# Padding two small tiles so that the tiles behind them begin at other addresses

## The chip, the cores and the metric

The program runs on one core of a Trainium2 chip. The metric is device time in microseconds, the median of several executions; lower is better. One further execution was recorded by the hardware profiler, and all rows below come from it.

## The reference, cut to what matters

```python
def reference(q, k, v, tau, moe_*, moe2_*):
    # 1. sparse attention: 4 batches x 8 heads, 576 tokens, head size 64
    scores = q @ k.T / 8;  keep scores >= rowmax - tau;  softmax;  attn @ v
    # 2. first layer, 2304 tokens x 512, inner width 1024
    x = ((x @ w1) * (x @ w2)) @ w3 @ w_out
    # 3. router and experts: 8 experts, inner width 1024
    P = exp(x @ w_gate - max); 8 rounds of normalising rows and columns
    out = sum over e of P[:, e] * (relu(x @ w1[e]) @ w2[e])
```

All arrays are float32.

## The kernel before, in words

**Arithmetic.** The large products run on TensorE in a float32 mode that takes one pass, and to keep the accuracy each operand is split into a high part and a low part. A product is three matmuls: high by high, high by low, low by high. Every one of these matmuls loads its own stationary operand of 128 by 128.

**Stages.** Attention takes some 390 us; the weights of the first layer are meanwhile converted and multiplied together (w3 by w_out) in its gaps. Then come 120 *units*. Units 0 to 23 are the first layer and units 24 to 119 the experts: three blocks of 768 tokens, eight experts, four parts of the inner width.

**One unit.** It has seven slots. In each slot `mm1` (L692) does six matmuls with 384 moving columns: stationary is a slice of the unit's converted first weights (`w1h`, `w1l`), moving is one of seven combinations of quarter blocks of x (`xh`, `xl`); the results go to the banks `px` and `py`. These are seven products in place of eight. The results are combined (`combine`), rectified and split into `hh` and `hl`, and one unit later the second product runs from a queue (`mm2`, L762) between the slots: for the experts 512 moving columns of `w2h` or `w2l` against stationary slices of `hh` and `hl`; for the first layer the roles are exchanged, with 256 or 512 moving columns. The result is added up in the banks `ye`.

**Preparation.** For the next unit `prep1` (L607 to L619) makes the converted first weights on GpSimd and ScalarE from a 512 KB load (`raw1`), and `prep2` makes `w2h` and `w2l` on ScalarE and VectorE. The order of all instructions is written out by hand. SyncE issues all transfers.

**Memory.** Tiles come from pools that are stacked from two ends. From the left: `const` (first `ntau`, then x), `moe` (sums of x, the even units' `w1h` and `w1l`, and `wt`), the converter's tiles during attention and in their place the `xh` and `xl`, then `moe1` (`prob`, `wg`, `ca`, `raw1`, the odd units' `w1h` and `w1l`, temporaries), then `moe2` (`raw2`, `acc`, `hh`, `hl`, `w2h`, `w2l`). From the right: all of attention's own tiles and the w3 by w_out tiles. Right-hand pools close before left-hand ones open over their place, and a tile opened there waits for the work on the tiles that it covers. Each tile begins at a multiple of 32 bytes in its partition, so `ntau`, which holds one number, takes 32 bytes. In units of bytes per partition, `prob` takes 576 and `wg` 128.

The two tiles that the change pads are `ntau`, L983 (the threshold, loaded once at L295, negated at L308, and read at L150 as the bias of a ScalarE operation in attention), and `wg`, L558 (the router's weights, loaded once at L559 and read at L843 as the moving operand of the 144 small matmuls of the router).

Of the kernel before, what the change touches and what calls it, by code (L numbers as in the profile page):

```python
# [9 lines left out]
F32 = mybir.dt.float32  # L10
# [10 lines left out]
DM, DFF, E = 512, 1024, 8  # L21
# [494 lines left out]
class Moe:  # L516
# [37 lines left out]
    def grow(self):  # L554

        pool = self.pool = self.odd = self.stack.enter_context(self.k.tc.tile_pool(name="moe1", bufs=1))
        self.p = pool.tile([128, NCH, E], F32, name="prob")
        self.wg = pool.tile([128, 4, E], F32, name="wg")  # L558
        self.nc.sync.dma_start(self.wg, self.k.wg)  # L559
        self.ca = pool.tile([128, 4, HT], F32, name="ca")  # L560
        self.load1(1)
# [413 lines left out]
@with_exitstack  # L975
def kernel(ctx, tc, qk, vv, tau, w1, w2, w3, wo, wg, e1, e2, out):
    k = Ctx()
    k.tc, k.nc = tc, tc.nc
    nc = tc.nc
    ctx.enter_context(tc.manual_schedule())  # L980
    const = ctx.enter_context(tc.tile_pool(name="const", bufs=1))
    dram = ctx.enter_context(tc.tile_pool(name="scratch", bufs=1, space=bass.MemoryType.DRAM))
    k.ntau = const.tile([128, 1], F32, name="ntau")  # L983
    k.tau = tau
    k.x = const.tile([128, 4, NTOK], F32, name="x")
    k.qk, k.vv, k.w3, k.wo, k.wg, k.w1, k.w2, k.out = qk, vv, w3, wo, wg, e1, e2, out
    k.w64 = {"a": w1, "b": w2}
    k.w34 = dram.tile([4, 128, 2, DM], F32, name="w34")
    k.wab = {n: dram.tile([4, 128, 1024], F32, name=f"w_{n}") for n in ("a", "b")}
    k.xk = dram.tile([3, 7, 128, 2 * HT], F32, name="x_low")  # L990
    k.wk = dram.tile([8, 2, 128, 7 * 256], F32, name="w_kept")
    attention(k)
# [44 lines left out]
```

## Time and profile before

| | |
|---|---|
| median of 3 executions | 2190.81 us (2189.88 to 2191.28) |
| the profiled execution, device time | 2189.07 us |
| its span, first to last instruction | 2187.3 us |
| busy share: PE, PEld, DVE, ACT, POOL | 98%, 86%, 58%, 43%, 48% |
| granted TensorE clock, mean | 1.000 |

PE stands for TensorE's matmuls, PEld for its weight loads, DVE for VectorE, ACT for ScalarE, POOL for GpSimd, SP for SyncE. A matmul's duration in the trace reaches from its start to the modelled end of its result, so that successive matmuls overlap; the distance of their starts tells the rate.

### The profile page before, as it was taken

The numbers are of one execution on the slowest core, as the hardware profiler recorded it, in microseconds if no ns is written. First come the engines' busy times: TensorE is split into PE (matmuls) and PEld (weight loads), VectorE is DVE, ScalarE is ACT, GpSimd is POOL, SyncE is SP. The second block draws the span as 40 slices with busy tenths as digits, with TensorE's granted clock in tenths as the row PEclk, the third lists the DMA queues.
The fourth block names the chain that finished last, engine by engine and source line by source line (L and its number), as shares of the span: only waits on it lengthen the run. The fifth ranks groups of instructions, "written<-read, shape, count | busy, mean of one in ns | idle before, by whom it ended". The sixth has DMA issues, their size and how long they took to land.

```text
span 2187.3 us, 31994 instructions
## 1 busy us (share of the span) xinstructions
PE 2150.1 (98%) x12496; PEld 1872.5 (86%) x12496; DVE 1274.8 (58%) x2122; ACT 948.0 (43%) x1770; POOL 1042.4 (48%) x1018
## 2 busy tenths in 40 slices
PE   7999999999999999999999999999999999999999
PEld 4666666899999899999998999999998999999998
DVE  7888888765555654454556445454546444545454
ACT  7888887442324333333334333333334333333332
POOL 6665657740003444444456545454456444444441
PEclk9999999999999999999999999999999999999999
DMA  4333442775552212121212121212112221212121
GB/s 154 105 128 123 133 139 86 260 264 188 222 199 105 78 58 77 59 77 59 77 58 93 72 77 58 77 59 77 64 72 73 92 72 63 77 59 78 58 77 39
DMA packets 64183, 218.09 MB, mean 100 GB/s; under 512 B 6944, under 2 KB 11040, under 8 KB 64032
## 3 DMA queue, kind: packets, MB, share of 16 engines
q1 hardware_dynamic: 64032, 216.05, 28.0%
q8 instruction: 98, 1.61, 0.3%
q14 instruction: 53, 0.43, 0.1%
HBM read 185.61 MB, written 30.41 MB: 99 GB/s over the span
## 4 chain that ended last, share of the span: by engine, by line
PE 90%; DVE 7%; ACT 2%; issue 1%; POOL 0%; DMA 0%; SPq 0%; ACTq 0%; DVEq 0%; POOLq 0%
PE ye L762 40%; PE py L692 22%; PE px L692 17%; PE s L143 4%; PE pv L241 2%; PE t L187 2%; DVE p L162 2%; DVE nmx L147 2%; PE w L474 1%; DVE cva L506 1%; PE py L843 0%; PE tt L198 0%; ACT e L155 0%; DVE cva L503 0%; PE rb L271 0%
## 5 line engine op out<-in xcount | busy, mean ns | idle before, releaser
L762 PE MATMUL ye<-w2l,hh 128*128 128x512 f32 x1152 | 450.6, 391 | 0.0
L762 PE MATMUL ye<-w2h,hl 128*128 128x512 f32 x1152 | 450.5, 391 | 0.0
L762 PE MATMUL ye<-w2h,hh 128*128 128x512 f32 x1152 | 449.6, 390 | 0.0
L757 ACT ACTIVATE hh<-c 128x384 fp32r<-128x384 f32 x288 | 151.2, 526 | 621.4 <-DVE c L736 621.4
L619 POOL TENSOR_TENSOR w1l<-wt,w1h 128x1024 fp32r<-128x1024 f32 x104 | 253.2, 2434 | 267.2 <-ACT w1h L616 267.1
L692 PE MATMUL py<-xh,w1h 128*128 128x384 f32 x960 | 322.6, 336 | 2.4 <-DVE c L736 1.2
L692 PE MATMUL py<-xh,w1l 128*128 128x384 f32 x960 | 322.1, 336 | 0.0
L692 PE MATMUL py<-xl,w1h 128*128 128x384 f32 x960 | 321.9, 335 | 0.0
L614 POOL TENSOR_TENSOR w1l<-raw,w1h 128x256 fp32r<-128x256 f32 x104 | 80.4, 773 | 471.2 <-ACT w1h L608 457.8
L762 PEld LDWEIGHTS ye<-w2h,hl 128*128 128x128 f32 x1152 | 216.2, 188 | 40.5
L762 PEld LDWEIGHTS ye<-w2l,hh 128*128 128x128 f32 x1152 | 216.3, 188 | 35.3 <-DVE w2l L642 0.3
L692 PE MATMUL px<-xh,w1h 128*128 128x384 f32 x720 | 242.0, 336 | 1.5 <-ACT p L716 1.5
L762 PEld LDWEIGHTS ye<-w2h,hh 128*128 128x128 f32 x1152 | 216.3, 188 | 30.7
L692 PE MATMUL px<-xl,w1h 128*128 128x384 f32 x720 | 241.6, 336 | 0.0
L692 PE MATMUL px<-xh,w1l 128*128 128x384 f32 x720 | 241.5, 335 | 0.0
L607 POOL TENSOR_TENSOR wt<-raw 128x512 f32<-128x512 f32 x104 | 140.8, 1354 | 198.0 <-DMA raw<-in_e 183.0
L758 DVE SCALAR_TENSOR_TENSOR hl<-c,hh 128x384 fp32r<-128x384 f32 x288 | 189.3, 657 | 9.5
L692 PEld LDWEIGHTS py<-xh,w1h 128*128 128x128 f32 x960 | 180.3, 188 | 14.8 <-DVE c L736 3.5
L692 PEld LDWEIGHTS py<-xl,w1h 128*128 128x128 f32 x960 | 180.3, 188 | 7.7
L736 DVE TENSOR_TENSOR c<-px,v 128x384 f32<-128x384 f32 x108 | 60.0, 556 | 212.8 <-PE px L692 212.7
L692 PEld LDWEIGHTS py<-xh,w1l 128*128 128x128 f32 x960 | 180.3, 188 | 0.0
L758 DVE SCALAR_TENSOR_TENSOR hl<-px,hh 128x384 fp32r<-128x384 f32 x96 | 53.4, 556 | 215.5 <-ACT hh L757 215.4
(144 smaller groups left out, 3941.0 us busy)
## 6 DMA issues: line engine op xcount, KB each, us to landing
raw<-in_e SPq DMA_DIRECT2D x192, 512.0 KB, 4.0
wraw<-in_w SPq DMA_DIRECT2D x32, 512.0 KB, 4.0
w1h<-w_kept SPq DMA_DIRECT2D x16, 896.0 KB, 5.2
w1l<-w_kept SPq DMA_DIRECT2D x16, 896.0 KB, 7.0
rq<-in_qk SPq DMA_DIRECT2D x15, 576.0 KB, 5.7
w_kept<-w1h SPq DMA_DIRECT2D x8, 896.0 KB, 8.2
w_kept<-w1l SPq DMA_DIRECT2D x8, 896.0 KB, 9.3
raw<-w SPq DMA_DIRECT2D x12, 512.0 KB, 3.6
```

What stands on the lines that cost most here:

```text
L143: nc.tensor.matmul(out[:, c, 0:KH], lhsT=q[rows, g, cols], rhs=kk[rows, g], start=True, stop=True)
L147: nc.vector.tensor_reduce(out=nmx[:, s % 18:s % 18 + 1], in_=ps[:, :, 0:288], axis=AX.XY, op=ALU.max, negate=True)
L162: nc.vector.scalar_tensor_tensor(out=ppool[g][:, i, 0:S].rearrange("p (a b) -> p a b", a=2), in0=ps[:, :, 0:288], scalar=thr[:, s % 18:s % ...
L187: nc.tensor.transpose(ps[:, c], p[:, 128 * c:128 * c + 128], k.ident)
L607: nc.gpsimd.tensor_tensor(out=t[:, 0:2], in0=raw[:, 1:3], in1=raw[:, 0:2], op=ALU.subtract)
L614: nc.gpsimd.tensor_tensor(out=wl[:, 0], in0=raw[:, 0], in1=f32(wh[:, 0]), op=ALU.subtract)
L619: nc.gpsimd.tensor_tensor(out=wl[:, 3:7], in0=t, in1=f32(wh[:, 3:7]), op=ALU.subtract)
L692: self.nc.tensor.matmul(out, lhsT=w[:, wi, o], rhs=x[xi][:, d], start=n == 0 and not adds, stop=n == 5, skip_group_check=True)
L736: tt(out=c, in0=src, in1=add, op=ALU.add)
L757: nc.scalar.activation(hi, src, AF.Relu)
L758: self.later.append(lambda: nc.vector.scalar_tensor_tensor(out=lo, in0=src, scalar=0.0, in1=f32(hi), op0=ALU.max, op1=ALU.subtract))
L762: self.queue.append((out.shape[-1], lambda: self.nc.tensor.matmul(out, lhsT=l, rhs=r, start=start, stop=stop, skip_group_check=True)))
```

## The change

The two tiles become wider, and the kernel goes on with the same leading part of each. `ntau` grows from 1 to 32 columns of four bytes, that is from 32 to 128 bytes, and `wg` from 4 by 8 to 6 by 8, from 128 to 192 bytes. Everything else is the same text.

```diff
@@ grow
         self.p = pool.tile([128, NCH, E], F32, name="prob")
-        self.wg = pool.tile([128, 4, E], F32, name="wg")
+        self.wg = pool.tile([128, 6, E], F32, name="wg")[:, 0:4]
         self.nc.sync.dma_start(self.wg, self.k.wg)
@@ tile_sparse_attention__then__two_moe_kernel
-    k.ntau = const.tile([128, 1], F32, name="ntau")
+    k.ntau = const.tile([128, 32], F32, name="ntau")[:, 0:1]
     k.tau = tau
```

## Rows read from the trace of the kernel before

**Rows 1.** The page: busy us (share of the span) and instructions of each engine.
```profile
PE 2150.1 (98%) x12496; PEld 1872.5 (86%) x12496; DVE 1274.8 (58%) x2122; ACT 948.0 (43%) x1770; POOL 1042.4 (48%) x1018
```

**Rows 2.** The page: the chain of waits, share of the span by engine and line.
```profile
PE 90%; DVE 7%; ACT 2%; issue 1%; POOL 0%; DMA 0%; SPq 0%; ACTq 0%; DVEq 0%; POOLq 0%
PE ye L762 40%; PE py L692 22%; PE px L692 17%; PE s L143 4%; PE pv L241 2%; PE t L187 2%; DVE p L162 2%; DVE nmx L147 2%; PE w L474 1%; DVE cva L506 1%; PE py L843 0%; PE tt L198 0%; ACT e L155 0%; DVE cva L503 0%; PE rb L271 0%
```

**Rows 3.** By stretch: length, busy us of PE, PEld, DVE, ACT, POOL, clock, DMA.
```profile
0.00:440.00 440.00, 407.99 (x3514) 286.00 (x3515) 369.88 (x727) 342.86 (x736) 282.70 (x419) 1.00 0.43 140
...
900.00:1300.00 400.00, 399.74 (x2011) 361.69 (x2010) 202.08 (x295) 144.82 (x246) 202.66 (x157) 1.00 0.21 73
```

**Rows 4.** Waits after 440 us, all engines, then PE alone: us in total, times, longest.
```profile
POOL w1l L614 <- ACT w1h L608: 452.5, 95, 5.4
POOL w1l L619 <- ACT w1h L616: 264.7, 97, 3.9
...
POOL wt L607 <- DMA raw<-in_e: 183.0, 1, 183.0
...
POOL w1l L614 <- DMA raw<-in_e: 13.4, 1, 13.4
...
PE py L692 <- DVE c L736: 0.5, 2, 0.3
PE px L877 <- DVE small L874: 0.4, 1, 0.4
```

**Rows 5.** Timeline, PE, the last matmuls: start us, duration us, engine, line, operation.
```profile
2179.64 0.39 PE L762 MATMUL ye<-w2h,hl 128*128 128x512 f32 x1
...
2183.04 0.39 PE L762 MATMUL ye<-w2h,hl 128*128 128x512 f32 x1
```

**Rows 6.** Timeline, PE, one slot of an expert unit and what follows it.
```profile
1226.99 0.33 PE L692 MATMUL py<-xh,w1h 128*128 128x384 f32 x1
...
1228.03 0.39 PE L762 MATMUL ye<-w2h,hl 128*128 128x512 f32 x1
```

**Rows 7.** Groups by line: xcount | busy us, mean ns of one | idle before.
```profile
L762 PE MATMUL ye<-w2l,hh 128*128 128x512 f32 x1152 | 450.6, 391 | 0.0
...
L762 PE MATMUL ye<-hh,w2l 128*128 128x256 f32 (+1 forms) x192 | 51.2, 338 | 0.9 <-DVE w2l L642 0.9
...
L692 PE MATMUL py<-xl,w1h 128*128 128x384 f32 x960 | 321.9, 335 | 0.0
...
L692 PE MATMUL px<-xl,w1h 128*128 128x384 f32 x720 | 241.6, 336 | 0.0
```

**Rows 8.** Timeline, DVE, three masks of attention in a row (the accumulators' reads left out).
```profile
86.90 0.81 DVE L162 SCALAR_TENSOR_TENSOR p<-s,thr,e 128x576 f32<-128x576 f32 x1
...
89.46 0.80 DVE L162 SCALAR_TENSOR_TENSOR p<-s,thr,e 128x576 f32<-128x576 f32 x1
...
92.17 0.81 DVE L162 SCALAR_TENSOR_TENSOR p<-s,thr,e 128x576 f32<-128x576 f32 x1
```

**Rows 9.** The page, DMA issues: count, KB each, median us from issue to landing.
```profile
raw<-in_e SPq DMA_DIRECT2D x192, 512.0 KB, 4.0
wraw<-in_w SPq DMA_DIRECT2D x32, 512.0 KB, 4.0
```

**Rows 10.** All instructions of L187 on PEld: count, ns min/median/max, first and last start.
```profile
L187 PEld LDWEIGHTS t<-ident,p x576: 137/141/231, 10.0 to 386.6; 128*128 128x128 f32 x192
```

**Rows 11.** Timeline, PE, first slot of unit 60 (even) and of unit 61 (odd).
```profile
1244.44 0.34 PE L692 MATMUL px<-xh,w1h 128*128 128x384 f32 x1
...
1245.49 0.33 PE L692 MATMUL py<-xh,w1h 128*128 128x384 f32 x1
...
1259.95 0.34 PE L692 MATMUL px<-xh,w1h 128*128 128x384 f32 x1
...
1260.99 0.34 PE L692 MATMUL py<-xh,w1h 128*128 128x384 f32 x1
```

## The prediction

> **What bounds the kernel now.** I began with the busy shares [rows 1] and the chain of waits [rows 2]. PE is busy for 98% of the span, and 79% of the chain are two lines: the second product L762 (40%) and the first product L692 (22% and 17%). The windows by stretch [rows 3] say where this holds: in a stretch of 400 us of the expert phase PE is busy for 399.74 us, at a granted clock of 1.00, which is the 2.4 GHz level, while DVE, ACT and POOL each stand idle for about half. In the first 440 us, mostly attention, PE has 408 us and DVE 370, and the DVE lines of the chain lie there. The waits after 440 us confirm it [rows 4]: the longest totals of PE itself are 0.5 and 0.4 us. So from some 390 us on, when the units begin, the time is the number of matmuls times the distance of their starts, and nothing else counts unless it becomes late enough to stop PE.
>
> That distance can be read. The last fifteen matmuls of 512 columns start between 2179.64 and 2183.04 us [rows 5]: 3.40 / 15 = 0.2267 us. Six matmuls of 384 columns take from 1226.99 to 1228.03 [rows 6]: 1.04 / 6 = 0.1733 us. The two differ by 53.4 ns for 128 columns, which is 128 ticks of 2.4 GHz (53.3 ns): a column costs one tick. At that rate 512 columns need 213.3 ns and 384 need 160.0, so each matmul has 13.3 ns on top, 32 ticks in either form.
>
> By the groups [rows 7] L692 has 3 x 960 + 3 x 720 = 5,040 matmuls and L762 has 3 x 1,152 + 3 x 192 = 4,032, together 9,072. The 32 ticks of all of them are 9,072 x 13.3 = 121 us. This is the only large sum that an address could reach.
>
> **The change part by part.** *Instructions.* None is added, removed or moved; no semaphore, queue or order changes. The one load of `ntau` and the one of `wg` bring the same bytes to the same number of partitions. Cost: nothing, and there is nothing that has to hide it.
>
> *Where tiles lie.* `ntau` takes 96 bytes more and `wg` 64. The text of the change says that every operand of the expert phase is then at a multiple of 256. Backwards, x, the even units' `w1h` and `w1l` and all `xh`, `xl` begin today at 256n - 96, that is at 160, and the tiles behind `wg` (the odd units' `w1`, `hh`, `hl`, `w2h`, `w2l`) at 256n - 160, that is at 96. Both are 32 past a multiple of 64. Attention's own tiles come from the other end and don't move, so of the first 390 us only the converter's tiles and the writes into x are touched.
>
> *Waits between old and new tiles.* A tile of `moe1` or `moe2` waits for the right-hand tiles under it. The left ones move by 96 or 160 bytes against these, and a border crossed would add or take away a wait at the change of stages. The sizes in the code, added up tile by tile, put the nearest borders 192 bytes apart (`ca` begins so far before the end of the right-hand `va`, `v` ends so far before the first `w3h`), and the shift is 160 at most: each left tile covers the same right tiles before and after. Cost: nothing, from both sides.
>
> *VectorE, ScalarE, GpSimd.* Their operands shift by 96 or 160 bytes. What they would gain or lose shows where the trace already has other addresses: the tile `p` of attention has rows of 580 numbers, 2,320 bytes, so three masks in a row write to places 16 bytes further each, modulo 64. They take 0.81, 0.80 and 0.81 us [rows 8]. Below nothing and above nothing the bound is the spread, 10 ns of 800, about 1%. In the expert phase these engines have half their time free [rows 3], and POOL's w1l waits on ACT for hundreds of microseconds in all [rows 4], so 1% of them doesn't reach PE. In the first 390 us the chain's DVE part is 7% of the span, 153 us, and mostly on tiles that stay; 1% of all of it would be 1.5 us. I take 0 and keep +-1.5 us.
>
> *Transfers.* They land 4.0 us after issue at either kind of address: `wraw` at 160 and `raw` of `in_e` at 96 [rows 9]. After 440 us POOL waits for a load twice, 183.0 and 13.4 us, while PE goes on without a gap [rows 4]. Shorter transfers are hidden; price 0.
>
> *TensorE, stationary operand.* Weight loads of `p` in the transposes start at the same 16-byte steps; the median of 576 is 141 ns beside a least of 137 [rows 10], so that the bound is some 4 ns of a load that lies beside a matmul. Even and odd units differ too: with moving x at 160, the stationary `w1` is at 160 or at 96, and the first slot of an even unit takes 1.05 us and of an odd one 1.04 [rows 11]. I take 0, with 10 ns a slot as the bound.
>
> *TensorE, moving operand.* Here the trace is blind: all large moving operands lie 32 past a multiple of 64 today. Modulo 256 they do differ, x at 160 and `w2` at 96, and both pay the same 32 ticks. Thus the price doesn't depend on which half of 128 bytes a stream begins in, and it isn't the length of the cut first piece, which would differ too (96 bytes to the next multiple of 256 against 160). From below the change could take all 32 ticks, -121 us; from above it is bounded by the first slots of units [rows 11]. I take 0, as the nearest rows (x against `w2`) show equal prices at unequal addresses.
>
> The Trainium skill has a figure that speaks against this choice, as a variant of rival A below. "TensorE: Matmul & The Clock Gate", section "Wait — 56ns, not 53.3ns?", gives about 2.5 ns per matmul above the columns for back-to-back matmuls at 2.4 GHz, where the rows here have 13.3. Whether its matmuls each had a weight load, it does not say; if addresses made the difference, 10.8 ns x 9,072 = 98 us would go.
>
> *The sum.* Profiled execution: span 2187.3 us and 1.8 around it, 2189.07; change 0, so 2189.1. The median shown is 1.7 us above this execution, so the time to be measured is **2190.8 us**, with its own range 2186.4 to 2195.2. (A difference under 0.2%, 4.4 us, can't be told from none.) Spread over the matmuls, 4.4 us is 0.48 ns each, a little over one tick.
>
> **The rivals.**
>
> *A, faster: the moving stream pays for its crooked start.* If the read begins with half of a 64-byte piece, 32 bytes or eight float32 columns are lost, 8 ticks = 3.3 ns per matmul: 9,072 x 3.3 = 30 us, time 2160.6. If all of the 32 ticks went, 2190.8 - 121 = 2070. For it: 32 ticks on every matmul that nothing in the profile explains, and no aligned case in the trace. Against it: the same 32 ticks at 160 and at 96, and that a fixed round number looks like the change of weights, which stays. The page cited above would put the time at 2093 as a variant of this rival. Chance 0.27, most of it nearer to the small price.
>
> *B, slower: streams that now lie alike collide.* After the change x and `w1`, `w2` and `hh` begin at the same place modulo 256 in all units, as x and the even units' `w1` do now. The even first slot is 10 ns longer than the odd one [rows 11]. If that is the price of equal residues after each change of operands, and it comes to hold wherever the stream switches from L762 to L692, four times in each of 120 units: 480 x 0.010 = 4.8 us, time 2195.6. It decides from 4.4 us on, 9.2 ns a switch. Against it: `w2` and `hh` lie alike already (both at 96) and pay no more. Chance 0.13, with a tail for collisions of DVE and ACT with PE that the trace can't show.
>
> *C, the change doesn't do what it says:* the allocator or the slices leave tiles where they are, or a slice brings a wait of its own. `ntau` and `wg` are read by waits that ended long before; the time would be 2190.8 as well, inside the forecast.
>
> **How the numbers follow.** Forecast with C 0.60, A 0.27, B 0.13. These give faster 0.27, same 0.60, slower 0.13. The range goes down past A's small price, 2160.6, to 2156, which leaves out A's larger prices, about 0.11, and up to 2200, past B's 2195.6, leaving out 0.04.
>
> **What would show it.** In the profile after, the fifteen last matmuls at 0.2267 us and the six of a slot at 0.1733 us as now would confirm the main step; starts closer than 0.2233 and 0.170 us would be A's small price, and 0.2133 and 0.160 all of it. B shows as an odd first slot of 1.05 us or more and slots longer than 1.04 throughout. The masks of attention at 0.81 us, PE idle time after 440 us still under 0.5 us per 400, and the load of `raw` at 4.0 us would confirm the small steps. The prediction is wrong if the distance of matmul starts moves by more than a tick, or if a stretch before 390 us changes by over 4 us.

## The result and the profile after

The changed kernel takes 2207.14 us (2206.87 to 2208.83, 4 runs) against 2190.79 us before: ratio 1.0077, 95% interval 1.0064 to 1.0090. It is 16.4 us slower; the forecast was no change, and the range ended at 2200.

The page of the kernel after, its span, busy time and chain, for [rows 1] and [rows 2]:

```profile
span 2207.0 us, 31994 instructions
PE 2169.6 (98%) x12496; PEld 1884.2 (85%) x12496; DVE 1272.2 (58%) x2122; ACT 947.9 (43%) x1770; POOL 1039.0 (47%) x1018
...
PE 90%; DVE 6%; ACT 2%; issue 1%; POOL 0%; DMA 0%; SPq 0%; ACTq 0%; POOLq 0%; DVEq 0%
```

PE does the same 12,496 matmuls and is busy for 19.5 us more; the other engines' sums are the same or a little less. The windows by stretch of the kernel after (columns as in [rows 3]):

```profile
0.00:440.00 440.00, 407.83 (x3502) 285.85 (x3502) 367.56 (x724) 341.13 (x733) 280.82 (x417) 1.00 0.43 140
900.00:1300.00 400.00, 399.81 (x1991) 359.95 (x1990) 201.41 (x293) 143.49 (x243) 202.88 (x158) 1.00 0.20 70
```

In the expert phase PE is as full as before (399.81 of 400 us) at the same clock, but 1,991 matmuls fit into 400 us in place of 2,011: 1% fewer. So no wait was added: the matmuls are farther apart. Where, the starts of units tell. First of the kernel before, then after, the first matmul of units 0, 40 and 118 (timeline, PE: start, duration):

```profile
388.52 0.45 PE L692 MATMUL px<-xh,w1h 128*128 128x384 f32 x1
...
933.76 0.34 PE L692 MATMUL px<-xh,w1h 128*128 128x384 f32 x1
...
2144.09 0.34 PE L692 MATMUL px<-xh,w1h 128*128 128x384 f32 x1
```

```profile
390.40 0.44 PE L692 MATMUL px<-xh,w1h 128*128 128x384 f32 x1
...
941.19 0.34 PE L692 MATMUL px<-xh,w1h 128*128 128x384 f32 x1
...
2163.56 0.34 PE L692 MATMUL px<-xh,w1h 128*128 128x384 f32 x1
```

From unit 40 to 118 it is 1222.37 against 1210.33 us: 12.04 us over 78 units, 0.154 us each, and from unit 0 to 40 another 5.55. The 1.88 us before unit 0 are not from the places of tiles: among the runs below, two that lose as much as this one start unit 0 at 388.36 and 388.58 us, and one that loses nothing at 390.38.

Inside a unit, the steady distance is the one of [rows 5]. The last sixteen starts of the kernel after:

```profile
2199.44 0.39 PE L762 MATMUL ye<-w2h,hl 128*128 128x512 f32 x1
...
2202.84 0.39 PE L762 MATMUL ye<-w2h,hl 128*128 128x512 f32 x1
```

3.40 / 15 = 0.2267 us, as before. What differs is the stretch behind each change from one product to the other. Unit 60, a run of nine matmuls of the second product and the slot that follows, first before, then after:

```profile
1246.54 0.39 PE L762 MATMUL ye<-w2h,hh 128*128 128x512 f32 x1
...
1248.59 0.33 PE L692 MATMUL px<-xh,w1h 128*128 128x384 f32 x1
1248.76 0.34 PE L692 MATMUL px<-xl,w1h 128*128 128x384 f32 x1
1248.93 0.34 PE L692 MATMUL px<-xh,w1l 128*128 128x384 f32 x1
1249.11 0.33 PE L692 MATMUL px<-xh,w1h 128*128 128x384 f32 x1
1249.28 0.33 PE L692 MATMUL px<-xl,w1h 128*128 128x384 f32 x1
1249.45 0.33 PE L692 MATMUL px<-xh,w1l 128*128 128x384 f32 x1
1249.63 0.33 PE L692 MATMUL py<-xh,w1h 128*128 128x384 f32 x1
...
1250.67 0.39 PE L762 MATMUL ye<-w2h,hh 128*128 128x512 f32 x1
```

```profile
1256.92 0.39 PE L762 MATMUL ye<-w2h,hh 128*128 128x512 f32 x1
...
1259.00 0.33 PE L692 MATMUL px<-xh,w1h 128*128 128x384 f32 x1
1259.17 0.34 PE L692 MATMUL px<-xl,w1h 128*128 128x384 f32 x1
1259.34 0.34 PE L692 MATMUL px<-xh,w1l 128*128 128x384 f32 x1
1259.52 0.35 PE L692 MATMUL px<-xh,w1h 128*128 128x384 f32 x1
1259.71 0.34 PE L692 MATMUL px<-xl,w1h 128*128 128x384 f32 x1
1259.88 0.34 PE L692 MATMUL px<-xh,w1l 128*128 128x384 f32 x1
1260.06 0.33 PE L692 MATMUL py<-xh,w1h 128*128 128x384 f32 x1
...
1261.10 0.39 PE L762 MATMUL ye<-w2h,hh 128*128 128x512 f32 x1
```

The nine take 2.08 us in place of 2.05, the six 1.06 in place of 1.04. Over all units from 42 to 118 the means are 2.081 against 2.052 and 1.066 against 1.042. From unit 40 on a unit has three such pairs (the runs of nine, nine and fourteen): 3 x (0.029 + 0.024) = 0.159 us, beside the 0.154 that a unit grew. A fourth pair loses nothing: the run of four that ends a unit takes 0.922 us in the mean after and 0.920 before, the first slot of the next unit 1.044 and 1.047. So not every change of product costs. A slot that follows another slot directly takes 1.040 us in the mean before and after (here 1249.63 to 1250.67 and 1260.06 to 1261.10), and of a run of fourteen only the first nine are late. The loss is a transient behind a change of product, that is, a stretch of longer distances after which the old distance comes back.

The slot of [rows 6] is one behind a change: the matmul ahead of it is of the second product. After the change the same slot, of unit 58, takes 1.07 us where it took 1.04. The line ahead of it before, then the slot after:

```profile
1226.76 0.39 PE L762 MATMUL ye<-w2l,hh 128*128 128x512 f32 x1
```

```profile
1237.18 0.33 PE L692 MATMUL py<-xh,w1h 128*128 128x384 f32 x1
...
1238.25 0.39 PE L762 MATMUL ye<-w2h,hl 128*128 128x512 f32 x1
```

The small steps, for [rows 4], [rows 8] and [rows 9], are as forecast: PE's own longest waits after 440 us are 0.6 and 0.4 us, a mask of attention takes 0.81 us, and the loads land as before:

```profile
raw<-in_e SPq DMA_DIRECT2D x192, 512.0 KB, 3.9
wraw<-in_w SPq DMA_DIRECT2D x32, 512.0 KB, 4.0
```

### The profile page after: what moved, and what is told of

The parts are those of the page before. It is cut to its first block, busy times and chain, and to the rows that moved or that the text cites. A ratio compares the mean times of both kernels' runs of the same rounds, so it can differ in the third digit from the quotient of the medians.

```text
span 2207.0 us, 31994 instructions
## 1 busy us (share of the span) xinstructions
PE 2169.6 (98%) x12496; PEld 1884.2 (85%) x12496; DVE 1272.2 (58%) x2122; ACT 947.9 (43%) x1770; POOL 1039.0 (47%) x1018
## 4 chain that ended last, share of the span: by engine, by line
PE 90%; DVE 6%; ACT 2%; issue 1%; POOL 0%; DMA 0%; SPq 0%; ACTq 0%; POOLq 0%; DVEq 0%
PE ye L762 40%; PE py L692 22%; PE px L692 17%; PE s L143 4%; PE pv L241 2%; PE t L187 2%; DVE p L162 2%; DVE nmx L147 1%; PE w L474 1%; DVE cva L506 1%; PE py L843 0%; PE tt L198 0%; ACT e L155 0%; PE rb L271 0%; DVE cva L503 0%
## 5 line engine op out<-in xcount | busy, mean ns | idle before, releaser
L762 PE MATMUL ye<-w2l,hh 128*128 128x512 f32 x1152 | 454.3, 394 | 0.0
L762 PE MATMUL ye<-w2h,hl 128*128 128x512 f32 x1152 | 454.1, 394 | 0.0
L762 PE MATMUL ye<-w2h,hh 128*128 128x512 f32 x1152 | 449.6, 390 | 0.0
L692 PE MATMUL py<-xh,w1h 128*128 128x384 f32 x960 | 324.0, 337 | 2.6 <-DVE ca L732 1.3
L692 PE MATMUL py<-xh,w1l 128*128 128x384 f32 x960 | 323.0, 336 | 0.0
L692 PE MATMUL py<-xl,w1h 128*128 128x384 f32 x960 | 322.6, 336 | 0.0
L762 PEld LDWEIGHTS ye<-w2h,hl 128*128 128x128 f32 x1152 | 216.2, 188 | 41.4
L762 PEld LDWEIGHTS ye<-w2l,hh 128*128 128x128 f32 x1152 | 216.1, 188 | 38.5
L692 PE MATMUL px<-xh,w1h 128*128 128x384 f32 x720 | 244.0, 339 | 1.2 <-ACT p L716 1.2
L762 PEld LDWEIGHTS ye<-w2h,hh 128*128 128x128 f32 x1152 | 216.6, 188 | 32.7
L692 PE MATMUL px<-xh,w1l 128*128 128x384 f32 x720 | 243.7, 338 | 0.0
L692 PE MATMUL px<-xl,w1h 128*128 128x384 f32 x720 | 242.9, 337 | 0.0
L692 PEld LDWEIGHTS py<-xh,w1h 128*128 128x128 f32 x960 | 180.3, 188 | 14.6 <-DVE c L736 3.4
L692 PEld LDWEIGHTS py<-xl,w1h 128*128 128x128 f32 x960 | 180.3, 188 | 8.1
L692 PEld LDWEIGHTS py<-xh,w1l 128*128 128x128 f32 x960 | 180.2, 188 | 0.0
```

Source lines behind the costliest of these rows:

```text
L692: self.nc.tensor.matmul(out, lhsT=w[:, wi, o], rhs=x[xi][:, d], start=n == 0 and not adds, stop=n == 5, skip_group_check=True)
L762: self.queue.append((out.shape[-1], lambda: self.nc.tensor.matmul(out, lhsT=l, rhs=r, start=start, stop=stop, skip_group_check=True)))
```

## The experiments

Each of the fourteen kernels differs from the kernel before by paddings alone. The table gives where the operands begin modulo 256, the time, and from the timeline of units 60 and 61 (even and odd) the length of the run of nine and of the slot behind it, each as the difference of two starts. Each ratio is to executions of the kernel before that were made beside that run (medians 2189.73 to 2190.86 us), not to the first row. The diffs are cut: they show, of each kernel against the kernel before, the lines that make a tile longer or add a gap, and the lines that these replace only with e1 and e2. A comment names the run for which a number or a line is meant.

| | x | w1 even | w1 odd | hh, hl | w2 | us | ratio to before, 95% | nine, 60 / 61 | slot, 60 / 61 |
|---|---|---|---|---|---|---|---|---|---|
| before | 160 | 160 | 96 | 96 | 96 | 2190.8 | | 2.05 / 2.05 | 1.04 / 1.04 |
| after | 0 | 0 | 0 | 0 | 0 | 2207.1 | 1.0077 (1.0064 to 1.0090) | 2.08 / 2.08 | 1.06 / 1.06 |
| e1 | 0 | 0 | 192 | 192 | 192 | 2189.9 | 1.0000 (0.9991 to 1.0009) | 2.05 / 2.05 | 1.04 / 1.04 |
| e2 | 160 | 160 | 160 | 160 | 160 | 2208.0 | 1.0084 (1.0067 to 1.0101) | 2.08 / 2.08 | 1.07 / 1.07 |
| e3 | 64 | 64 | 64 | 64 | 64 | 2207.3 | 1.0081 (1.0066 to 1.0096) | 2.09 / 2.08 | 1.06 / 1.07 |
| e4 | 0 | 0 | 32 | 32 | 32 | 2188.7 | 0.9994 (0.9985 to 1.0003) | 2.05 / 2.04 | 1.05 / 1.05 |
| e5 | 160 | 160 | 96 | 160 | 96 | 2205.5 | 1.0077 (1.0061 to 1.0092) | 2.10 / 2.09 | 1.04 / 1.04 |
| e6 | 160 | 160 | 96 | 96 | 160 | 2195.0 | 1.0024 (1.0015 to 1.0034) | 2.06 / 2.06 | 1.07 / 1.04 |
| e7 | 160 | 160 | 160 | 96 | 96 | 2190.5 | 1.0003 (0.9994 to 1.0013) | 2.05 / 2.06 | 1.04 / 1.04 |
| e8 | 0 | 0 | 128 | 128 | 128 | 2202.5 | 1.0059 (1.0044 to 1.0074) | 2.07 / 2.05 | 1.07 / 1.05 |
| e9 | 0 | 0 | 0 | 32 | 32 | 2190.7 | 1.0002 (0.9993 to 1.0010) | 2.05 / 2.05 | 1.04 / 1.04 |
| e10 | 160 | 160 | 96 | 96 | 224 | 2205.8 | 1.0067 (1.0053 to 1.0080) | 2.09 / 2.09 | 1.07 / 1.05 |
| e11 | 160 | 160 | 96 | 96 | 128 | 2209.7 | 1.0084 (1.0068 to 1.0099) | 2.08 / 2.10 | 1.07 / 1.04 |
| e12 | 0 | 0 | 192 | 0 | 0 | 2204.1 | 1.0062 (1.0048 to 1.0075) | 2.08 / 2.07 | 1.07 / 1.04 |
| e13 | 160 | 192 | 192 | 192 | 192 | 2187.1 | 0.9988 (0.9979 to 0.9997) | 2.04 / 2.05 | 1.05 / 1.04 |
| e14 | 160 | 128 | 128 | 128 | 128 | 2201.8 | 1.0048 (1.0035 to 1.0060) | 2.04 / 2.04 | 1.06 / 1.06 |

**e1, the first padding alone.**

```diff
-    k.ntau = const.tile([128, 1], F32, name="ntau")
+    k.ntau = const.tile([128, 32], F32, name="ntau")[:, 0:1]
```

> Only the 96 bytes behind ntau: x, xh, xl and the even units' w1 begin at 0 modulo 256, all tiles behind wg (odd units' w1, hh, hl, w2h, w2l) at 192. Theory L (a stream that begins at a multiple of 64 pays more after a change of streams, whatever the other stream's place): all are multiples of 64, so as slow as the changed kernel, about 2207 us. Theory E (the price comes where the streams of the first and of the second product begin at the same place modulo 256): places differ (0 and 192), so as the kernel before, about 2191 us. Theory M (only the moving x of the first product counts): about half of the loss, near 2199 us.

2189.94 us, the time of before. All left-hand tiles moved together by 96 bytes, to multiples of 64, and nothing changed. Theories L and M fall, E stands.

**e2, the second padding alone.**

```diff
-        self.wg = pool.tile([128, 4, E], F32, name="wg")
+        self.wg = pool.tile([128, 6, E], F32, name="wg")[:, 0:4]
```

> Only the 64 bytes behind wg: x, xh, xl and the even units' w1 stay at 160 modulo 256, all tiles behind wg begin at 160 too. Theory L: nothing begins at a multiple of 64, so as before, about 2191 us. Theory E: all streams begin at the same place, so as slow as the changed kernel, about 2207 us. Theory M: as before, 2191 us.

2207.95 us, all of the loss, though no operand lies at a multiple of 64. The first and the last start of the slot behind the run of nine in its unit 60, and the first of the next slot:

```profile
1257.90 0.33 PE L692 MATMUL px<-xh,w1h 128*128 128x384 f32 x1
...
1258.97 0.33 PE L692 MATMUL py<-xh,w1h 128*128 128x384 f32 x1
```

1.07 us, as late as after. So the 64 bytes behind `wg` make the loss: they take away the 64 bytes by which the second product's operands lay off from x. The 96 behind `ntau` do nothing.

**e3, all at 64.**

```diff
+    k.ntau = const.tile([128, 48], F32, name="ntau")[:, 0:1]
+        self.wg = pool.tile([128, 6, E], F32, name="wg")[:, 0:4]
```

> Padding of 160 bytes behind ntau and 64 behind wg: every operand of the expert phase begins at 64 modulo 256 in place of 0. Theory L: multiples of 64, slow, about 2207 us. Theory E: the same place for all, slow, about 2207 us. If only a multiple of 128 or 256 is bad, as before, 2191 us.

2207.34 us: a third common place (0, 160, 64) with the same loss. It is not the multiple of 256.

**e4, x at 0 and the rest at 32.**

```diff
+    k.ntau = const.tile([128, 32], F32, name="ntau")[:, 0:1]
+        self.wg = pool.tile([128, 7, E], F32, name="wg")[:, 0:4]
```

> Padding of 96 bytes behind ntau and 96 behind wg: x, xh, xl and the even units' w1 at 0 modulo 256, all tiles behind wg at 32. Theory L: the first product's moving stream is at a multiple of 64 and pays, the second product's streams don't: half of the loss, about 2199 us, with the slots after a change long and the second product's matmuls as before. Theory E: places differ, 2191 us. Theory M: about 2199 us, as L.

2188.70 us, as E said and not as L and M; the 1.4 us under the kernel before are within the interval.

**e5 and e6, one operand of the second product alone.** In e5 `acc` grows by 64 bytes and a gap of 192 stands behind `hl`; in e6 there is a gap of 64 bytes behind `hl`.

```diff
+                if u == 1:
+                    self.gap = self.pool2.tile([128, 48], F32, name="gap")   # e6: 16
+        self.acc = self.pool2.tile([128, 6 * DM + 16], F32, name="acc")[:, 0:6 * DM].rearrange("p (a b) -> p a b", a=6)   # e5 alone
```

> Of all tiles of the expert phase only hh and hl (the second product's stationary operands in the expert units) are moved from 96 to 160 modulo 256, where x begins; w2h, w2l and the odd units' w1 stay at 96, x at 160. The runs so far say that the loss comes where the tiles of the two products begin at the same place modulo 256. Theory H (the weight load of one product that runs beside a matmul of the other collides: hh against x): slow, about 2207 us, or the half of it that the second product showed, 2199. Theory S (the two moving streams: w2 against x): as before, 2191 us. Theory W (odd w1 against x): as before, 2191 us.

> Only w2h and w2l (the second product's moving operands in the expert units) are moved from 96 to 160 modulo 256, where x begins; hh, hl and the odd units' w1 stay at 96. Theory S (moving against moving): slow, about 2207 us. Theory H (hh against x): as before, 2191 us, or even a little off it, as w2 and hh now begin at different places. Theory W: as before, 2191 us.

Both are slower, 2205.53 and 2195.03 us, but not in the way that H or S had it. The last sixteen starts of e5, then of e6:

```profile
2196.35 0.39 PE L762 MATMUL ye<-w2h,hl 128*128 128x512 f32 x1
...
2199.85 0.40 PE L762 MATMUL ye<-w2h,hl 128*128 128x512 f32 x1
```

```profile
2185.55 0.39 PE L762 MATMUL ye<-w2h,hl 128*128 128x512 f32 x1
...
2188.99 0.40 PE L762 MATMUL ye<-w2h,hl 128*128 128x512 f32 x1
```

3.50 / 15 = 0.2333 us and 3.44 / 15 = 0.2293: with `hh` and `w2` 64 bytes apart the second product never comes back to 0.2267. That is a second effect, of the pair that runs together, and it makes nearly all of e5's loss: its slots take 1.04 us. In e6 the slot behind a change is late in even units (1.07, where x, w1 and w2 are alike) and not in odd ones (1.04, where w1 is apart).

**e7, all but hh and w2 like x.**

```diff
+        self.wg = pool.tile([128, 6, E], F32, name="wg")[:, 0:4]
+        self.acc = self.pool2.tile([128, 6 * DM + 48], F32, name="acc")[:, 0:6 * DM].rearrange("p (a b) -> p a b", a=6)
```

> Padding of 64 bytes behind wg, taken back by 192 bytes behind acc: the odd units' w1, the temporaries, raw1, raw2 and acc begin at 160 modulo 256 like x; hh, hl, w2h and w2l begin at 96. Theory W (the first product's own two streams, x against w1): odd units slow, about 2199 us. Theory D (places where ScalarE, VectorE, GpSimd and the DMA write, rather than TensorE's streams): slow, about 2207 us. Theories S and H: as before, 2191 us.

2190.51 us: it is e2 with `hh`, `hl`, `w2h`, `w2l` moved on by 192 bytes, which is 64 back modulo 256, and the whole loss is gone. The odd units' w1, the temporaries and the tiles that loads write into have no part by themselves: W and D fall.

**e8, x at 0, the rest at 128.**

```diff
+    k.ntau = const.tile([128, 32], F32, name="ntau")[:, 0:1]
+        self.wg = pool.tile([128, 10, E], F32, name="wg")[:, 0:4]
```

> Padding of 96 bytes behind ntau and 192 behind wg: x and the even units' w1 begin at 0 modulo 256, all tiles behind wg at 128. If what counts is the place modulo 256, the places differ and the time is as before, 2191 us, or up to 2 us better as with a difference of 32; if it is the place modulo 128, they are the same and it is slow, 2207 us.

2202.50 us, between the two answers. Even units' slots behind a change are late (1.07), the runs of nine are less so (2.07 and 2.05), and in odd units, where x and w1 lie 128 apart, every slot is long, 1.053 us in the mean, also those that follow no change. So 128 is neither the same place nor a free one.

**e9, the repair.**

```diff
+    k.ntau = const.tile([128, 32], F32, name="ntau")[:, 0:1]
+        self.wg = pool.tile([128, 6, E], F32, name="wg")[:, 0:4]
+        self.acc = self.pool2.tile([128, 6 * DM + 8], F32, name="acc")[:, 0:6 * DM].rearrange("p (a b) -> p a b", a=6)
```

> The changed kernel with hh, hl, w2h and w2l moved on by 32 bytes (8 more numbers behind acc): x and all w1 at 0 modulo 256, hh, hl, w2h, w2l at 32. Theory P (the price is that of the start places of the two products' operands against each other, and shows as long distances after each change of product): the second product's places differ from the first's, so the whole loss goes, and as with a difference of 32 before some 20 ns a unit are gained on the kernel before: 2188.5 us. Theory A (alignment of the first product's operands to 256 is itself bad): 2207 or at least 2199 us.

2190.66 us. The changed kernel with 32 bytes more behind `acc` has no loss, though x and all w1 still lie at multiples of 256; theory A falls. The 2 us that I expected on top did not come.

**e10 and e11, w2 off hh by 128 and by 32.**

```diff
+                if u == 1:
+                    self.gap = self.pool2.tile([128, 32], F32, name="gap")   # e11: 8
```

> The kernel before with w2h and w2l moved on by 128 bytes: hh, hl at 96 and w2 at 224 modulo 256, x at 160. With w2 64 ahead of hh or 64 behind it the second product's matmuls had no steady 0.2267 us any more (0.229 and 0.233). If the places count modulo 128, hh and w2 are alike again, the steady distance is 0.2267 us and the time near 2191 us; if modulo 256, the distance stays above 0.229 us and the time is 2195 us or more.

> The kernel before with w2h and w2l moved on by 32 bytes: hh, hl at 96 and w2 at 128 modulo 256, x at 160. If 32 bytes are enough to keep the moving stream and the weight load apart, the steady distance falls below 0.2267 us, by up to the 13.3 ns on top of the columns: as low as 2145 us. If equal places are the best for a pair that runs together, it lies above 0.2267 us and the time is 2193 to 2206 us. If the 32 ticks on top don't come from places, 0.2267 us and 2191 us.

2205.75 and 2209.65 us. The last sixteen starts of e10, then of e11:

```profile
2196.25 0.39 PE L762 MATMUL ye<-w2h,hl 128*128 128x512 f32 x1
...
2199.73 0.40 PE L762 MATMUL ye<-w2h,hl 128*128 128x512 f32 x1
```

```profile
2200.23 0.39 PE L762 MATMUL ye<-w2h,hl 128*128 128x512 f32 x1
...
2203.73 0.40 PE L762 MATMUL ye<-w2h,hl 128*128 128x512 f32 x1
```

3.48 / 15 = 0.2320 us and 3.50 / 15 = 0.2333. For `w2` against `hh` the same place is the best of the five tried (0: 0.2267, +64: 0.2293, +128: 0.2320, +32 and -64: 0.2333), and none goes below the 32 ticks on top.

**e12, the odd units' w1 taken out.**

```diff
+    k.ntau = const.tile([128, 32], F32, name="ntau")[:, 0:1]
+        self.acc = self.pool2.tile([128, 6 * DM + 16], F32, name="acc")[:, 0:6 * DM].rearrange("p (a b) -> p a b", a=6)
```

> The changed kernel with only the odd units' w1 (and raw1, raw2, acc and the temporaries) 64 bytes back, at 192 modulo 256; x, the even units' w1, hh, hl, w2h, w2l at 0. Theory P, with the part of the first product asking for x, w1 and w2 alike all three (as the runs with hh or w2 moved showed by parity of the unit): the odd units' slots lose their long distances (some 75 ns a unit less), the even units' and the second product's stay: about 2202.5 us. If w1 has no part, 2207 us.

2204.13 us. The slot behind a change in unit 60, then in unit 61 (first start, and the start of what follows):

```profile
1256.23 0.33 PE L692 MATMUL px<-xh,w1h 128*128 128x384 f32 x1
...
1257.30 0.33 PE L692 MATMUL py<-xh,w1h 128*128 128x384 f32 x1
...
1271.89 0.34 PE L692 MATMUL px<-xh,w1h 128*128 128x384 f32 x1
...
1272.93 0.34 PE L692 MATMUL py<-xh,w1h 128*128 128x384 f32 x1
```

1.07 us in the even unit and 1.04 in the odd one; the runs of nine stay late in both (2.08 and 2.07). The first product's part of the loss asks for w1 in the common place as well.

**e13 and e14, x alone apart.** Paddings behind the last of the sums `s`, behind `wt` and behind `wg` put every operand but x 32 bytes off to either side; one line more in the text moves L692 to L693 and L762 to L763.

```diff
+        self.xs.append(pool.tile([128, 2 * HT + 8], F32, name="s3")[:, 0:2 * HT].rearrange("p (a b) -> p a b", a=2))   # e14: 56
+        self.wg = pool.tile([128, 7, E], F32, name="wg")[:, 0:4]   # e14: 5
+        t = self.even.tile([128, 1024 + 56], F32, tag="wt", name=f"wt{u}", bufs=1)[:, 0:1024].rearrange("p (a b) -> p a b", a=4)   # e14: 8
```

> x, xh, xl stay at 160 modulo 256; all w1 (even and odd units), hh, hl, w2h, w2l begin at 192, 32 bytes further on. Theory P (the loss needs x, w1 and the second product's operands alike, all of them): no loss, and in all units what the odd units had with such a difference of 32 (second product at its steady distance from the first matmul on, about 32 ns a unit less than before): about 2187.5 us. Theory R (w1 like hh and w2 is enough for a loss at the change of product, x has no part): 2200 us or more.

> As the run before with the sign turned: x, xh, xl at 160 modulo 256; all w1, hh, hl, w2h, w2l at 128, 32 bytes less. Theory P: no loss of the kind of the changed kernel, 2187 to 2193 us; if the sign doesn't matter, as the run before, about 2187.5 us. Theory R: 2200 us or more.

e13 takes 2187.08 us, ratio 0.9988 (0.9979 to 0.9997): faster than the kernel before by some 2.6 us, with an interval that only just leaves out 1, and where expected. Its run of nine in unit 60:

```profile
1246.22 0.39 PE L763 MATMUL ye<-w2h,hh 128*128 128x512 f32 x1
...
1248.26 0.34 PE L693 MATMUL px<-xh,w1h 128*128 128x384 f32 x1
```

2.04 us, nine times the steady distance: the second product has no transient left. e14 takes 2201.79 us, against theory P. It has no transient of the second product either (2.04 us), but the first product is slow throughout, as in this slot of unit 60 that follows another slot:

```profile
1258.93 0.34 PE L693 MATMUL py<-xh,w1h 128*128 128x384 f32 x1
...
1259.99 0.39 PE L763 MATMUL ye<-w2h,hh 128*128 128x512 f32 x1
```

1.06 us where such a slot of the kernel before takes 1.04 (1249.63 to 1250.67 above). R names the right time, but for another reason: not the change of product, the pair x and w1 itself. The sign counts: with w1 32 bytes ahead of x the pair is free, with w1 32 behind it isn't.

## Why the prediction was wrong

**What bounds the kernel: right.** The loss is matmul distance and nothing else; PE's waits, the other engines, the loads and the waits between old and new tiles came out as costed, at nothing. Spread over the 9,072 matmuls, as the sum did with its 4.4 us, the loss is 1.8 ns each; in fact it lies on some of them only.

**The step that failed: "TensorE, moving operand ... I take 0, as the nearest rows (x against `w2`) show equal prices at unequal addresses".** The step asked what one stream pays for its own address and read that off the steady distances. e1, e2 and e3 show that the own address costs nothing: three common places are equally slow, and a common shift of 96 bytes changes nothing. What counts is where the operands of the two products begin *against each other*. The equal 32 ticks at 160 and at 96 did not bear on that. The kernel before has x 64 bytes ahead of `hh` and `w2`, a place that costs little, and the padding behind `wg` takes just these 64 bytes away (e2 makes the loss, e7 undoes it).

**Rival B had the right place for the loss, but the wrong pairs and the wrong evidence.** The price does sit behind switches of the stream, and it comes when operands lie alike. But B named x with `w1` and `w2` with `hh`. In e7 both pairs are alike in every unit, nothing is lost (ratio 1.0003), and the first slots take 1.042 us in the mean in even and in odd units: what costs is that the second product lies like the first. B's only figure, the 10 ns of the even first slot [rows 11], 4.8 us in all, did not spread but went: the even first slots take 1.053 us in the mean before and 1.044 after, the odd ones 1.041 and 1.044. Measured are 24 ns for a slot behind a change, three times a unit and not four, and 29 ns for the run of nine behind the change back, which B left out: 0.154 us a unit, 12 us from unit 40 to 118. That B pointed to slower was thus in part luck. B's "against it", that `w2` and `hh` lie alike already and pay no more, was true and beside the point: these two run together, and e5, e6, e10 and e11 show that for them alike is best.

**The bounds.** What was missing is the transient as a term of its own. I took the first slots of units for an upper bound of every change, "10 ns a slot", and they stand behind the one change that loses nothing. Of the signs, the fifteen last matmuls at 0.2267 us came as a confirmation would have, since they are far from any change; the six of the slot in [rows 6], at 1.07 / 6 = 0.178 us in place of 0.1733, say that the forecast is wrong. The runs of nine in the profile before already take 2.05 us and not 2.04, so that a transient of some 10 ns behind each change stood there to be read, and e13 shows that it could go.

**Rival A** (a faster stream from a straight start) has nothing for it: with the moving operands of both products at 0, 64 and 160 (after, e3, e2) the steady distances are 0.2267 and 0.1733 us as before. The figure of the Trainium skill set beside it ("TensorE: Matmul & The Clock Gate", section "Wait — 56ns, not 53.3ns?": about 2.5 ns above the columns) is not reached here: no placement tried has a steady distance with less than 13.3 ns on top.

**What stays open.** Shown is which placements lose and where in the trace; the mechanism inside TensorE's reads is not. The whole loss comes when x, w1, hh and w2 all begin alike modulo 256; the slots' part of it also comes in the even units when w2 alone is moved by 32, 64 or 128 (e11, e6, e10) or all of the second product lies 128 from the first (e8). One regularity, read off the runs afterwards and not forecast, covers the slots behind a run of nine in all units where x and w1 begin alike: they go by where `w2` begins against x, and not by `hh` (e5, e6). With `w2` at the same place, 64 or 128 bytes ahead, or 32 behind, they take 1.065 to 1.070 us in the mean (after, e2, e3, e6, e8, e10, e11, e12); with `w2` 32 ahead or 64 behind, 1.041 to 1.046 (before, e1, e4, e5, e7, e9). Why these and not those stays open, and no rule of mine gives the runs of nine as well. That places count modulo 256 rests on e7 alone: there the second product's operands lie 256 bytes further on than before, and the even units' runs of nine and the slots behind them are the same within 1 ns. That no other engine has a part in it is argued from one place, the last slot of the kernel after, whose six starts run from 2192.89 to 2193.96 us, 1.07 us, as late as any; the window over it:

```profile
2192.89:2193.96 1.07, 1.07 (x8) 1.07 (x7) 0.00 (x0) 0.00 (x0) 0.00 (x0) 1.00 0.00 0
```

DVE, ACT, POOL and the DMA engines stand still there. It was not tried with TensorE alone.

## What to carry to other kernels

Before a padding that aligns everything, list where the operands begin against each other: here a common shift was free, and equal places for two products that alternate cost 0.8%. Look at the starts right behind each change of operands, not only at the steady distance, since a transient of a few ns per matmul, three pairs a unit, makes microseconds. And move one operand at a time by 32 bytes: such an edit costs one number in a tile's shape, and here it ranged from 0.9988 to 1.0084 of the time.

## What the runs showed of the hardware that I had not expected

- The distance of matmul starts depends on the places of moving and stationary operand against each other: 0.2267 us for 512 columns with both alike, 0.2293 to 0.2333 with the moving one 64 or 128 ahead, 32 ahead or 64 behind. For 384 columns 0.1733 alike, with the moving one 64 ahead or 32 behind, and 0.1767 (1.06 / 6) with it 32 ahead.
- After a change of operands the distance takes up to nine matmuls to settle, and what that costs depends on the operands before the change: between the even units of the kernel before and of e6 only `w2` lies elsewhere, and the slot behind a run of nine takes 1.043 us in the mean and 1.065.
- The pattern is reproducible to a nanosecond: e1, with all tiles shifted together, has the slots and runs of the kernel before within 1 ns in the mean.
